# One of three phase additions moved from VectorE to GpSimd in a two-layer attention and gMLP kernel, with eight more units on VectorE

## The chip, the core and the metric

The kernel runs on one core of one Trainium2 chip. The core has TensorE (matmuls; it writes PSUM, a memory of 8 banks of 128 x 512 fp32), ScalarE (activation functions), VectorE and GpSimd (elementwise work; GpSimd reads and writes SBUF alone) and SyncE, which issues the DMAs here. Each engine has its own instruction queue and works through it in order; semaphores order the engines against each other. The metric is the device time of one execution in microseconds (us). Three runs of the kernel before took 1680.24, 1680.46 and 1686.99 us; the median is 1680.46.

## The reference

Two layers, each an attention block (A) and a gMLP block (B), on x of 2048 rows by 512. There are 32 heads of 16 channels, and all heads share one K and one V (multi-query attention).

```python
def _A_ref(x, wq, wk, wv, wo):
    q = (x @ wq).reshape(B, S, H, Dh).transpose(0, 2, 1, 3)     # H = 32, Dh = 16, S = 2048
    k = x @ wk
    v = x @ wv
    scores = jnp.einsum('bhqd,bkd->bhqk', q, k) * Dh ** (-0.5)
    p = _softmax(scores, axis=-1)
    o = jnp.einsum('bhqk,bkd->bhqd', p, v)
    return o.transpose(0, 2, 1, 3).reshape(B, S, H * Dh) @ wo

def _B_ref(x, w_in, w_sp, b_sp, w_out):
    z = _gelu(jnp.einsum('bsd,df->bsf', x, w_in))
    z1 = z[..., :Fh].copy()
    z2 = _layernorm(z[..., Fh:], axis=-1)
    g = jnp.einsum('ts,bsf->btf', w_sp, z2) + b_sp[None, :, None]
    return jnp.einsum('bsf,fd->bsd', z1 * g, w_out)

x = x + _A_ref(_layernorm(x), ...); x = x + _B_ref(_layernorm(x), ...)   # twice
```

The attention takes an exponential of 2 x 32 x 2048 x 2048 scores. That is the bulk of the work.

## The kernel before

**Units and blocks.** In each layer the queries and heads are cut into 32 groups (`GROUPS`), each with 512 columns of query and head times 4 row strips j of the PE array. A group runs over 16 key tiles of 128 keys. One group with one key tile is a *unit*: four *blocks* of 128 keys x 512 columns of scores.

**Units on ScalarE.** Most units go the plain way. TensorE makes scores into one of two slots of PSUM, of three and of two banks (`push_slot`, L837). ScalarE takes the exponential of a whole slot, 128x1536 or 128x1024, into the tile `P_ring` (L863). TensorE multiplies with V and adds up into bank 6 (L882).

**Units on VectorE.** The other units, `ON_DVE` counts them per group, are spread through the slots (`plan`, `apart`) and made by VectorE without an exponential (`block_dve`, L951). TensorE writes one block into a side bank (5 or 7). VectorE evacuates it as int16: the score, plus a bias, clipped at 0, is read as the bits of a bf16, which is a rough power of two (L970, four times a unit, into row r0 of the tile `big`). To make it smoother, five such numbers with different offsets (*phases*) are averaged. The first is r0 itself. The other four are r0 with an integer added: VectorE adds for r2 (L981, 128x2048), then for r1 and r3 in one instruction from r0 and r2 (L983, 128x4096), and last for r4 (L985, 128x2048). TensorE then multiplies each phase with V, scaled by that phase's weight, onto the same bank 6 (`sum_units`, L1001, five times four matmuls a unit, in the order of phases 0, 2, 1, 3, 4). The rows of `big` go round a ring of six (`NRING`), five to a unit, so a unit's additions overwrite rows that the unit before it filled, and wait until TensorE has read them.

**Other work.** At the end of a group VectorE evacuates bank 6 (L1059, or L1050 and L1056 with a partial sum), and turns, divisions (L1031 on VectorE, the products L1041 mostly on GpSimd), the output projection and its addition to X (L1089) follow; then layer norms (L737, L738, L742, with GpSimd's L724 and L726 for the reciprocal square root), the gMLP's input projection (L1181, L1206), the GELUs on ScalarE (L1216, L1245, L1177, L1203), the spatial mixing (L1307, L1349, products L1354 on VectorE or GpSimd). TensorE also gets filler matmuls on zeros (L671, L663) where it would stand idle. At the start of layer 1 there is a stretch in which keys, values and the first queries of the new layer are made (`ln_tiles`, `kv_tiles`, `q_slot`, evacuated by VectorE on L759, L777, L810).

**What sets the order.** Every operation is recorded with an engine, a cost in us, a priority and what it reads and writes. `_Graph.schedule` then plays the program through with these costs, as a list scheduler: an engine that is free takes the ready operation with the lowest priority number. What comes out is a fixed order for each engine's queue; semaphore waits are put in from the reads and writes. So a cost in the code changes no duration, only the order. The phase additions have priority 6.98 (`P_PH`), late among VectorE's work, the evacuations L970 have 0.2 (`P_R`), the multiplications with V have 1. The table `URGENCY` adds small numbers to the priorities of named portions of the program ("unit.0.13 pe" is TensorE's part of the VectorE units while pass 13 of layer 0 is open).

Of the kernel before, what the change touches and what calls it, by code (L numbers as in the profile page):

```python
# [6 lines left out]
FP32 = mybir.dt.float32  # L7
# [39 lines left out]
    "/b_front.0.0.4": -2, "/b_front.0.0.4 pe": 2, "/b_front.0.15.1/ln_tiles.0.15.1": -2, "/b_front.0.6.2 pe": 2,  # L47
    "/b_front.0.8.4/ln_tiles.0.8.4": 0.5, "/b_front.0.8.4/norm_z2.0.6.2": -1.5, "/b_front.0.8.4/norm_z2.0.8.4": -2,
    "/b_front.1.12.3 pe": 1.5, "/b_front.1.15.1/ln_tiles.1.15.1": -1.5, "/b_front.1.4.2 pe": -2,
    "/b_front.1.6.2 pe": 1, "/b_front.1.8.4/ln_tiles.1.8.4": 1, "/finish_group.0.1": 3, "/finish_group.0.2": -3,  # L50
    "/finish_group.0.26": -2, "/finish_group.0.29 pe": -1, "/finish_group.0.30 pe": 0.5, "/finish_group.0.31": 3,
    "/finish_group.1.11": -3, "/finish_group.1.27": -3, "/finish_group.1.28 pe": -3, "/finish_group.1.29 pe": 2,
    "/finish_group.1.30 pe": -3, "/finish_group.1.31 pe": 3, "/kv_tiles.0.2.2 pe": 1, "/kv_tiles.1.12.4 pe": -2,
    "/kv_tiles.1.2.2 pe": 1.5, "/kv_tiles.1.4.2 pe": 1, "/kv_tiles.1.6.2": -3, "/kv_tiles.1.6.2 pe": 1,
    "/kv_tiles.1.8.4 pe": 3, "/ln_tiles.0.6.2": -1, "/ln_tiles.1.0.2 pe": -2, "/ln_tiles.1.2.2 pe": -1,
    "/ln_tiles.1.6.2 pe": -1.5, "/ln_tiles.1.8.4 pe": -2, "/mix_late.1.0.2 pe": -3,
    "/mix_late.1.0.2/add_to_x.1.3": -3, "/mix_late.1.0.6": -3, "/mix_stage.0.0.1 pe": -1.5,
    "/mix_stage.0.1.2 pe": -1, "/mix_stage.0.1.3 pe": -1.5, "/mix_stage.1.0.1 pe": -3, "/mix_stage.1.1.3 pe": 0.5,
    "/q_slot.0.11.4 pe": 2, "/q_slot.0.15.4 pe": 1, "/q_slot.0.4.4 pe": -2, "/q_slot.1.12.4 pe": -1.5,
    "/q_slot.1.13.4 pe": 1, "/q_slot.1.15.4 pe": -1.5, "/q_slot.1.3 pe": 2, "/q_slot.1.4.4 pe": -3,  # L60
    "/q_slot.1.8.4 pe": -3, "/turn_tile.1.14.3 pe": 2, "/wo_tiles.0.14.1 pe": -3, "/wo_tiles.0.2.2 pe": -2,
    "/wo_tiles.1.12.2 pe": -2, "/wo_tiles.1.4.2 pe": -3, "/wo_tiles.1.6.2 pe": -2, "unit.0.10 pe": 1,
    "unit.0.11": -2, "unit.0.12 pe": -2, "unit.0.14 pe": -1, "unit.0.16 pe": 3, "unit.0.18 pe": 2,
    "unit.0.23 pe": -3, "unit.0.25 pe": 3, "unit.0.28 pe": -1.5, "unit.0.29": 1, "unit.0.29 pe": 0.5,
    "unit.0.31 pe": -2, "unit.0.33 pe": 1.5, "unit.0.35": -1.5, "unit.0.35 pe": -3, "unit.0.4": -2,
    "unit.0.40 pe": -0.5, "unit.0.9": -1.5, "unit.1.56": 1.5, "unit.1.58": -1, "unit.1.58 pe": 1, "unit.1.59": -1,
    "unit.1.60 pe": -3, "unit.1.62 pe": 3, "unit.1.63 pe": 1, "unit.1.64 pe": -2, "unit.1.65 pe": 1,
    "unit.1.66 pe": -2, "unit.1.67 pe": -1.5, "unit.1.68": -0.5, "unit.1.68 pe": -2, "unit.1.69 pe": -1,
    "unit.1.70": 1.5, "unit.1.71 pe": 1, "unit.1.72 pe": 1, "unit.1.74 pe": 1.5, "unit.1.75 pe": -3,
    "unit.1.77 pe": 1, "unit.1.79 pe": 2, "unit.1.80 pe": 2, "unit.1.83 pe": 0.5, "unit.1.85 pe": 0.5,  # L70
# [423 lines left out]
def bass_interleave_layers__grouped_kv_mqa__mixer_gmlp__prompt_kernel(  # L494
# [46 lines left out]
    mhalf = G.sb([P, 1], FP32, "mhalf")  # L541
    X = G.sb([P, NT, D], BF16, "X")
# [177 lines left out]

    def rstd(n, ve, rs, mv, i0, ni, per_tile, prio):

        for a, b in ([(i, i + 1) for i in range(i0, i0 + ni)] if per_tile else [(i0, i0 + ni)]):
            op("pool", lambda e, a=a, b=b: e.tensor_scalar(ve[:, a:b], mv[:, a:b, 1], LN_EPS, None, op0=ALU.add),  # L724
               0.25, r=[("mv" + n, i) for i in range(a, b)], w=[("ve" + n, i) for i in range(a, b)], prio=prio)
            op("pool", lambda e, a=a, b=b: e.tensor_tensor(rs[:, a:b], ve[:, a:b],  # L726
                                                           mhalf[:, 0:1].to_broadcast([P, b - a]), ALU.pow),
               0.3 + 0.2 * (b - a), r=[("ve" + n, i) for i in range(a, b)] + ["mhalf"],
               w=[("rs" + n, i) for i in range(a, b)], prio=prio)

    @portion
    def ln_tiles(t0, n, xT, keys, per_tile, prio=5, by_dma=False):
# [19 lines left out]
        while t < t0 + n:  # L752
            m = 1 if per_tile else min(2, t0 + n - t)
            tk = _Task()
            products(tk, m * KD, lambda e, k, t=t, tk=tk: e.transpose(  # L755
                bank16(tk.bank)[:, k * P:(k + 1) * P], xn[:, (t + k // KD) % CT, (k % KD) * P:(k % KD + 1) * P],
                ident[:]), lambda k, t=t: [("xn", (t + k // KD) % CT), "ident"], prio, 0.065, per=8)
            c0 = (t if xT is xnTA else t % CT) * P
            dve(lambda e, c0=c0, m=m, tk=tk: e.tensor_copy(  # L759
                xT[:, :, c0:c0 + m * P].rearrange("p kd (t q) -> p t kd q", q=P),  # L760
                bank16(tk.bank)[:, 0:m * KD * P].rearrange("p (t kd q) -> p t kd q", t=m, kd=KD)),
                0.16 + 0.27 * m, [tk], [x for y in range(t, t + m) for x in keys(y)], prio)
            t += m
# [3 lines left out]
    def kv_tiles(t0, n, pr, pr_v):  # L767
# [8 lines left out]
        for a in range(2):  # L776
            dve(lambda e, a=a: e.tensor_scalar(kT_rep[:, a, t0 * P:t0 * P + w], bank32(t1.bank)[:, 0:w], rows[:, a:a + 1],  # L777
                                               None, op0=ALU.mult), 0.15 + 0.135 * n, [t1, "rows"],
                [("K", a, t) for t in range(t0, t0 + n)], pr + 0.05 * a)
# [15 lines left out]
    @portion  # L795
    def q_slot(si, pr=3):

        t0, n, g = GROUPS[2 * si]
        m, w = CT // n, n * P
        tk = _Task()  # L800

        def mk(e, k):
            u, kd = k // KD, k % KD
            c = g // 2 * m + u
            mul = side4 if n > 1 else PE_FULL
            return mul(e, bank32(tk.bank)[:, u * w:(u + 1) * w], wq_r[:, kd, c * P:(c + 1) * P],
                       xnTA[:, kd, t0 * P:t0 * P + w], kd == 0, kd == KD - 1)
        products(tk, m * KD, mk, lambda k: [("xa", k % KD, t) for t in range(t0, t0 + n)] + ["wq"], pr,
                 us=w * MM + 0.01, mode=2 if n > 1 else 0)
        dve(lambda e: e.tensor_scalar(qT[:, si % NQ, :], bank32(tk.bank), Q_SCALE, None, op0=ALU.mult), 0.69, [tk],  # L810
            [("q", si % NQ)], pr)
# [92 lines left out]
    spread = {"todo": [], "summed": []}  # L904

    def plan(passes):

        at = main["n"] + len(main["blocks"])
        for no, (hg, kts, on_dve) in enumerate(passes):
            n = 4 * (len(kts) - len(on_dve))  # L910
            for d, kt in enumerate(on_dve):
# [3 lines left out]
                                       "first": None, "summed": False})  # L915
# [15 lines left out]
    def tiles_free(x):  # L931
# [7 lines left out]
        return all(phr["owner"].get(r, {"summed": True})["summed"] for r in need)  # L939

# [10 lines left out]
    def block_dve(x, j, slot_op):  # L951
# [25 lines left out]
        if k == 3:  # L977
# [7 lines left out]
            dve(lambda e: e.tensor_scalar(ph16[:, r4, :], ph16[:, r0, :], float(PH_A[4]), None, op0=ALU.add), 0.63, base,  # L985
                BIG(r4), P_PH)
# [58 lines left out]

    def evac_first(hg):
        dve(lambda e: e.tensor_copy(acc[:, hg, :], bank32(PVB)), 0.69, ["pvb"], [ACC(hg)], 0)

    def evac_add(hg):
        dve(lambda e: e.tensor_tensor(acc[:, hg, :], bank32(PVB), acc[:, hg, :], ALU.add), 0.69, ["pvb", ACC(hg)],  # L1050
            [ACC(hg)], 0)

    def evac_last(gi, with_acc):
        par = grp["n"] % 2
        if with_acc:
            dve(lambda e: e.tensor_tensor(oT[:, par, :], bank32(PVB), acc[:, gi, :], ALU.add), 0.69,  # L1056
                ["pvb", ACC(gi)], [("oT", par)], 0)
        else:
            dve(lambda e: e.tensor_copy(oT[:, par, :], bank32(PVB)), 0.69, ["pvb"], [("oT", par)], 0)  # L1059
# [43 lines left out]
    def attn_first(t0, n, on_dve):  # L1103

        plan([(q_of(gi), range(t0, t0 + n), [t0 + k for k in on_dve]) for gi in range(NFIRST)])
        for gi in range(NFIRST):
# [10 lines left out]
    def attn_rest():  # L1117
        plan([(q_of(gi), range(NT), UNITS[ON_DVE[now['layer']][gi]]) for gi in range(NFIRST, len(GROUPS))])
        for gi in range(NFIRST, len(GROUPS)):
# [5 lines left out]
    def group_done(gi, with_acc):  # L1125
# [3 lines left out]
        if gi == NFIRST - 1:  # L1129
# [100 lines left out]
    def gelu_rest():  # L1230
# [11 lines left out]
        for t0, n in Z1_LATE:  # L1242
# [4 lines left out]
            us = 0.0  # L1247

# [114 lines left out]
    def sums_lead(n, chain):  # L1363
# [38 lines left out]
    LATE4 = 4  # L1402
    TURN_US = 7.0
# [6 lines left out]
    NFIRST = 2 * CHUNKS[0][1]  # L1410
    ATT = (((0, 2), (2, 6), (8, 8)), ((0, 2), (2, 2), (4, 2), (6, 2), (8, 8)))
    FIRST_DVE = ({2: (2,), 8: (2, 4)}, {8: (3, 5)})
# [10 lines left out]
    ON_DVE = [[0] * NFIRST + [int(c) for c in s] for s in (  # L1423
        "4344433443423243434344233232",
        "4344443434333433344432333231")]

    for layer in range(2):
        now["layer"] = layer
        phr["base"] = 8 - NRING
        for t0, n in KEYS:  # L1430
# [11 lines left out]
            for a0, an in ATT[layer]:  # L1442
                if a0 + an == t0 + n:
                    attn_first(a0, an, FIRST_DVE[layer].get(a0, ()))
# [42 lines left out]
```

## Time and profile before

| | |
|---|---|
| Median of 3 runs | 1680.46 us |
| Profiled execution | 1682.92 us, span of its instructions 1680.1 us |
| Granted TensorE clock, mean | 0.984 |
| ScalarE: first exponential begins | 13.14 us |
| ScalarE: last GELU ends | 1630.05 us |
| Longest waits of ScalarE for scores | 24.0 and 8.3 us, at 802 and 841 us (start of layer 1) |
| Units on VectorE | 202 (808 evacuations of one block) |
| Blocks on ScalarE | 3,288, in 1,316 exponentials |
| Table loads on ScalarE | 14 of 1.283 us |
| GpSimd products L1041, 128x128 | 112 of 0.40 us median, longest 1.26 |

An instruction is named by its line (a helper's line stands for all that calls it), its engine, its operation, and out<-in by tile and shape. PE is TensorE's matmuls, PEld its weight loads, DVE VectorE, ACT ScalarE, POOL GpSimd. A row of a group ends with its busy time, the mean duration of one, and the idle time of the engine just before them with what ended it. A row of a stretch gives, after its start and end, length and busy time of PE, PEld, DVE, ACT and POOL with counts, then the granted clock and the DMA's share. A row in order of time has start and duration first.

### The profile page before, as it was taken

Reading aid. Unit: us, or ns where it says so; the run is one execution under the profiler, and the core shown is the slowest. Engines: PE = TensorE matmul, PEld = TensorE weight load, DVE = VectorE, ACT = ScalarE, POOL = GpSimd, SP = SyncE. Lnnn points to the kernel's source line nnn. Section 1 sums busy time; section 2 is a strip of 40 time slices with the busy share of each in tenths; the row PEclk is TensorE's granted clock in tenths of the full one; section 3 lists DMA queues with packets and bytes.
Section 4 is the critical chain, followed back from the end, with each engine's and each line's share of the span. In section 5 each row is a group of like instructions: output and inputs, shape, how many; then the busy total and the mean of one; then the engine's idle time right before and its main releaser. Section 6 shows DMA issues by size and latency. Waiting matters only on the chain.

```text
span 1680.1 us, 45324 instructions
## 1 busy us (share of the span) xinstructions
PE 1599.8 (95%) x20268; PEld 530.8 (32%) x20281; DVE 1465.9 (87%) x2384; ACT 1563.2 (93%) x1360; POOL 156.6 (9%) x261
## 2 busy tenths in 40 slices
PE   8999999989999998999999999999999999999999
PEld 3222222233333322334532222223333333323344
DVE  8899999997899998877878998999989999887677
ACT  7899999999999999999479999999999999999970
POOL 2000010000000010000430100000110000010012
PEclk9899999999999998999998999999999999989999
DMA  6100010002311230444511100100013203215555
GB/s 186 23 14 14 8 23 8 20 9 76 80 27 43 81 63 17 126 143 141 156 46 23 18 8 11 23 8 14 11 58 74 48 31 83 73 36 142 171 162 146
DMA packets 173266, 102.70 MB, mean 61 GB/s; under 512 B 135056, under 2 KB 145680, under 8 KB 173072
## 3 DMA queue, kind: packets, MB, share of 16 engines
q1 hardware_dynamic: 173072, 99.81, 23.2%
q8 instruction: 158, 2.59, 0.7%
q14 instruction: 36, 0.29, 0.1%
HBM read 36.34 MB, written 31.46 MB: 40 GB/s over the span
## 4 chain that ended last, share of the span: by engine, by line
ACT 80%; PE 17%; DVE 2%; issue 0%; POOL 0%; DMA 0%; SPq 0%; ACTq 0%
ACT P_ring L863 78%; PE ps_all L637 4%; PE ps_all L631 4%; PE ps_all L837 4%; PE ps_all L1001 2%; PE ps_all L882 2%; ACT z2n L1216 1%; PE ps_all L671 1%; PE ps_all L663 0%; ACT L863 0%; ACT L1216 0%; DVE big L970 0%; DMA X<-in_A_x_dram 0%; PE ps_all L755 0%; DVE xn L742 0%
## 5 line engine op out<-in xcount | busy, mean ns | idle before, releaser
L863 ACT ACTIVATE P_ring<-ps_all 128x1536 bf16<-128x1536 f32 (+1 forms) x1316 | 1493.6, 1347 | 63.3 <-PE ps_all L837 62.5
L837 PE MATMUL ps_all<-qT,kT_rep 32*128 32x512 bf16 x4096 | 612.7, 389 | 65.5 <-ACT P_ring L863 54.0
L970 DVE TENSOR_SCALAR big<-ps_all 128x512 int16<-128x512 f32 x808 | 535.4, 685 | 79.3 <-PE ps_all L837 73.0
L837 PEld LDWEIGHTS ps_all<-qT,kT_rep 32*128 32x128 bf16 x4096 | 150.7, 91 | 609.0 <-ACT P_ring L863 496.5
L1001 PE MATMUL ps_all<-big,V_ph 128*32 128x512 bf16 x4040 | 337.4, 388 | 2.7 <-DVE big L985 1.3
L882 PE MATMUL ps_all<-P_ring,V_aug 128*32 128x512 bf16 x3288 | 306.6, 390 | 1.9 <-DVE oT L1059 1.6
L983 DVE TENSOR_SCALAR big<-big 128x4096 int16<-128x4096 int16 x202 | 246.3, 1219 | 5.2 <-PE ps_all L1001 4.7
L1041 POOL TENSOR_TENSOR o_norm<-o_rows,rden 128x128 bf16<-128x128 bf16 x112 | 57.4, 532 | 1010.3 <-DVE rden L1031 973.7
L981 DVE TENSOR_SCALAR big<-big 128x2048 int16<-128x2048 int16 x202 | 138.4, 685 | 5.8 <-PE ps_all L1001 3.6
L985 DVE TENSOR_SCALAR big<-big 128x2048 int16<-128x2048 int16 x202 | 137.9, 692 | 3.1 <-PE ps_all L1001 2.7
L1001 PEld LDWEIGHTS ps_all<-big,V_ph 128*32 128x32 bf16 x4040 | 90.5, 95 | 133.3 <-issue 66.8
L882 PEld LDWEIGHTS ps_all<-P_ring,V_aug 128*32 128x32 bf16 x3288 | 80.9, 95 | 143.8 <-issue 106.8
L637 PE MATMUL ps_all<-xnTA,z2n 128*32 128x512 bf16 x1344 | 95.5, 386 | 0.0
L671 PE MATMUL ps_all<-ones,zeros 128*32 128x512 bf16 x1076 | 94.5, 395 | 0.0
L1089 DVE TENSOR_TENSOR X<-ps_all,X 128x512 bf16<-128x512 f32 x64 | 44.0, 687 | 25.1 <-PE ps_all L637 15.2
L637 PE MATMUL ps_all<-w_in_r,xo 128*32 128x448 bf16 x960 | 62.9, 355 | 0.1
L724 POOL TENSOR_SCALAR ve<-mv 128x1 f32<-128x1 f32 (+3 forms) x40 | 17.3, 434 | 458.8 <-DVE mv L738 355.1
L637 PE MATMUL ps_all<-xo,w_in_r 128*32 128x512 bf16 (+2 forms) x1120 | 57.3, 327 | 0.3 <-DVE big L970 0.2
L1307 DVE TENSOR_TENSOR big<-ps_all,big 128x512 f32<-128x512 f32 x56 | 38.3, 686 | 21.3 <-PE ps_all L637 20.7
L1181 DVE CAST z2n<-ps_all 128x448 bf16<-128x448 f32 x60 | 37.2, 621 | 14.4 <-PE ps_all L637 13.7
L1354 POOL TENSOR_TENSOR z1c<-big,z1c 128x512 bf16<-128x512 f32 (+1 forms) x47 | 45.5, 983 | 36.4 <-DVE big L1349 35.7
L637 PE MATMUL ps_all<-z1c,z2n 128*32 128x512 bf16 x672 | 48.1, 382 | 0.1
(96 smaller groups left out, 1032.7 us busy)
## 6 DMA issues: line engine op xcount, KB each, us to landing
gp_scratch<-big SPq DMA_DIRECT2D x112, 256.0 KB, 2.0
big<-gp_scratch SPq DMA_DIRECT2D x98, 256.0 KB, 3.3
big<-gp_scratch SPq DMA_DIRECT2D x28, 128.0 KB, 2.7
out_dram<-X SPq DMA_DIRECT2D x16, 128.0 KB, 1.7
w_in_r<-in_B_w_in_dram SPq DMA_DIRECT2D x1, 1792.0 KB, 7.3
X<-in_A_x_dram SPq DMA_DIRECT2D x3, 512.0 KB, 6.5
bsp<-in_B_b_sp_dram SPq DMA_DIRECT2D x8, 128.0 KB, 3.5
w_out_r<-in_B_w_out_dram SPq DMA_DIRECT2D x1, 896.0 KB, 5.0
```

What stands on the lines that cost most here:

```text
L631: return e.matmul(out, w, mv, start=start, stop=stop)
L637: ins = e.matmul(out[32 * j:32 * j + 32, :], w[:, 32 * j:32 * j + 32], mv, tile_position=(0, 32 * j), start=start, stop=stop)
L671: ins = e.matmul(bank32(PVB)[32 * j:32 * j + 32, :], zeros[:, 0:32], mv, tile_position=(0, 32 * j), start=False, stop=False)
L837: return e.matmul(out, kT_rep[32 * j:32 * j + 32, a, u[1] * P:(u[1] + 1) * P], qT[32 * j:32 * j + 32, q, :], tile_position=(32 * j, 0), st ...
L863: return e.activation(P_ring[:, s0:s0 + n, :], bank32(b0, n).rearrange("p (k q) -> p k q", k=n), ACTF.Exp, scale=E_SCALE)
L882: ins = e.matmul(bank32(PVB)[32 * j:32 * j + 32, :], V_aug[:, kt, :], P_ring[:, s, :], tile_position=(0, 32 * j), start=first, stop=last)
L970: o = dve(lambda e: e.tensor_scalar(ph16[:, tiles[0], j * QC:(j + 1) * QC], bank32(tk.bank), PH_BIAS, 0.0, op0=ALU.add, op1=ALU.max), 0.66 ...
L981: dve(lambda e: e.tensor_scalar(ph16[:, r2, :], ph16[:, r0, :], float(PH_A[2]), None, op0=ALU.add), 0.63, base, BIG(r2), P_PH)
L983: dve(lambda e: e.tensor_scalar(two_rows(tiles[1], tiles[3]), two_rows(r0, r2), float(PH_A[1]), None, op0=ALU.add), 1.16, base + BIG(r2), ...
L985: dve(lambda e: e.tensor_scalar(ph16[:, r4, :], ph16[:, r0, :], float(PH_A[4]), None, op0=ALU.add), 0.63, base, BIG(r4), P_PH)
L1001: ins = e.matmul(bank32(PVB)[32 * j:32 * j + 32, :], V_ph[:, a, kt, :], big[:, tiles[a], j * QC:(j + 1) * QC], tile_position=(0, 32 * j), ...
L1041: op("pool" if on_pool else "dve", lambda e, b0=b0, nb=nb, dst=dst: e.tensor_tensor(dst, src()[:, b0:b0 + nb, :, 0:DH], rden[:, par, b0:b0 ...
```

## The change

- The last addition of a unit (row r4) is put on GpSimd instead of VectorE where the group's index is under 30 (`POOL_TO`), except for every 99th unit (`POOL_EVERY`); it is given to the scheduler with a cost of 5.0 us (`POOL_US`) and priority 4. 200 of 210 are moved.
- The counts in `ON_DVE` change: 3 units more in layer 0 and 5 in layer 1 are on VectorE, 8 in all, so 32 blocks fewer go through ScalarE's exponential.
- At the start of layer 1, the evacuations for the first two row tiles (two turned inputs, two of K, two of Q; `evac` with `ON_ACT`) are made by ScalarE as copies with a scale instead of by VectorE.
- `URGENCY` is another table throughout (125 entries in place of 101).
- Rewritten without another effect here: `attn_first` takes the range of its groups as arguments, `part_sums` names where partial sums lie (the first four groups alone, as before), `DUMMY` is off.

In the program built from the changed source, the last GELU of z2 in layer 0 and the late GELUs of z1 stand together, with 12 table loads on ScalarE. Lines move: L970 is now L991, L981 L1002, L983 L1004, L985 L1007, L863 L877, L837 L851, L1001 L1024.

```diff
+    def evac(t0, own, us, r, w, prio, dst, src, scale=None):
+
+        if own and t0 in ON_ACT[now["layer"]]:
+            op("act", lambda e: e.activation(dst(), src(), ACTF.Copy, scale=1.0 if scale is None else scale()), us - 0.1,
+               r=r + ["exp_table"] if DUMMY else r, w=w, prio=prio)
+        elif scale is None:
+            dve(lambda e: e.tensor_copy(dst(), src()), us, r, w, prio)
+        else:
+            dve(lambda e: e.tensor_scalar(dst(), src(), scale(), None, op0=ALU.mult), us, r, w, prio)
...
+    def on_gpsimd(x):
+
+        pool_n["n"] += 1
+        gi = x["gi"]
+        return gi < POOL_TO and pool_n["n"] % POOL_EVERY != 0
...
-            dve(lambda e: e.tensor_scalar(ph16[:, r4, :], ph16[:, r0, :], float(PH_A[4]), None, op0=ALU.add), 0.63, base,
-                BIG(r4), P_PH)
+            on_pool = on_gpsimd(x)
+            op("pool" if on_pool else "dve", lambda e: e.tensor_scalar(ph16[:, r4, :], ph16[:, r0, :], float(PH_A[4]), None,
+                                                                       op0=ALU.add), POOL_US if on_pool else 0.63,
+               r=base, w=BIG(r4), prio=4 if on_pool else P_PH)
...
+    DUMMY = False
+    POOL_US, POOL_EVERY, POOL_TO = (5.0, 99, 30)
+    ON_ACT = ((), (0,))
...
-        "4344433443423243434344233232",
-        "4344443434333433344432333231")]
+        "4444433443324343442444332332",
+        "4344444444343443434434333230")]
```

## The prediction

> **What bounds the kernel now.** I read the page's busy shares and its chain of waits first, then the groups, then who waits for whom, then busy time by stretch.
>
> ```profile
> span 1680.1 us, 45324 instructions
> PE 1599.8 (95%) x20268; PEld 530.8 (32%) x20281; DVE 1465.9 (87%) x2384; ACT 1563.2 (93%) x1360; POOL 156.6 (9%) x261
> ...
> ACT 80%; PE 17%; DVE 2%; issue 0%; POOL 0%; DMA 0%; SPq 0%; ACTq 0%
> ...
> L863 ACT ACTIVATE P_ring<-ps_all 128x1536 bf16<-128x1536 f32 (+1 forms) x1316 | 1493.6, 1347 | 63.3 <-PE ps_all L837 62.5
> L970 DVE TENSOR_SCALAR big<-ps_all 128x512 int16<-128x512 f32 x808 | 535.4, 685 | 79.3 <-PE ps_all L837 73.0
> L983 DVE TENSOR_SCALAR big<-big 128x4096 int16<-128x4096 int16 x202 | 246.3, 1219 | 5.2 <-PE ps_all L1001 4.7
> L981 DVE TENSOR_SCALAR big<-big 128x2048 int16<-128x2048 int16 x202 | 138.4, 685 | 5.8 <-PE ps_all L1001 3.6
> L985 DVE TENSOR_SCALAR big<-big 128x2048 int16<-128x2048 int16 x202 | 137.9, 692 | 3.1 <-PE ps_all L1001 2.7
> ```
>
> The chain is ScalarE's exponentials (L863). TensorE's 95% holds the fillers of L671 (94.5 us), which nobody waits for. ScalarE's whole wait for scores is 62.5 us, of which 11.1 is the start and 24.0 and 8.3 are the change of layers; only 19.1 us is scattered.
>
> ```profile
> ACT P_ring L863 <- PE ps_all L837: 62.5, 29, 24.0
> ```
>
> ```profile
> 95.00:360.00 265.00, 250.73 (x3073) 76.06 (x3076) 248.51 (x383) 264.83 (x235) 16.16 (x32) 1.00 0.08 14
> 920.00:1200.00 280.00, 264.09 (x3269) 79.77 (x3270) 262.88 (x401) 278.04 (x245) 20.84 (x32) 0.99 0.08 14
> ```
>
> Here ScalarE (fourth busy time) is at 99% and VectorE (third) at 94%. So VectorE has 6% to spare there: lateness on it soon becomes lateness of TensorE and then of ScalarE.
>
> **What is removed from ScalarE.** Eight units are 32 blocks of 128x512. L863 holds 3,288 blocks in 1493.6 us, 0.454 us each: -14.5 us. The changed order holds 12 table loads for 14, because the last GELU of layer 0 now stands beside the other GELUs: 2 x 1.283 = -2.6 us. Six copies come to ScalarE (at the start of layer 1), 0.59 us each by the GELU row of the same shape (L1203, 592 ns), in place of VectorE's 0.69. They lie in the 24.0 us wait, where ScalarE is idle; the exponential's table load now stands behind them. Together I take 0, bounds -1 and +1.3 (one load bare). Without further effects: 1680.1 - 14.5 - 2.6 = 1663.0.
>
> **VectorE and TensorE.** 192 of 202 last additions leave VectorE: 192 x 0.692 = -132.9 us. Eight units bring 4 x 0.685 + 0.685 + 1.219 = 4.64 each, +37.2. The six copies leave: -3.2. VectorE: 1465.9 - 98.9 = 1367 us. TensorE gets 160 phase matmuls more and 32 others fewer, of which four run at once: 128 x 0.388 / 4 = +12.4 us, covered by the fillers; bare, 12.4 is the price. The new urgencies reorder VectorE and TensorE: I take 0, with the scattered 19.1 us as the bound both ways. What stands behind the additions in GpSimd's queue (112 products of L1041, 40 pairs of L724 and L726) may come one addition later. GpSimd idles 973.7 us ahead of L1041, whose results go to transposes, not to the exponentials; VectorE waited only 7.6 us in all for L726. Cost 0 under that cover, and once per pair, 40 x 2 = 80 us, on VectorE without it.
>
> **How long an addition takes on GpSimd.** No row shows it. Bounds:
>
> ```profile
> L1354 POOL TENSOR_TENSOR z1c<-big,z1c 128x512 bf16<-128x512 f32 x26 | 31.7, 1228 | 28.1 <-DVE big L1349 28.0
> L1354 POOL TENSOR_TENSOR z1c<-big,z1c 128x256 bf16<-128x256 f32 x21 | 13.8, 679 | 8.3 <-DVE big L1349 7.6 <-DVE mv L738 0.6
> ...
> L706 POOL MEMSET V_ph<- 128x2560 bf16 x1 | 2.2, 2231 | 0.1
> ...
> L704 POOL MEMSET V_aug<- 128x512 bf16 x1 | 0.5, 524 | 0.0
> ```
>
> The memsets grow by (2231 - 524) / 2048 = 0.83 ns an element: 1.80 us for 2048. The products, undisturbed 1154 and 667 ns, by 1.90 ns with 0.18 fixed: 4.07 us. A product reads two tensors and the addition one; half the slope gives 0.18 + 2048 x 0.95 = 2.13 us, nearer to the memset. I take 2.13. GpSimd is then busy 156.6 + 426 us, far from full. (The Trainium skill, GPSIMD Engine Reference, Engine selection, calls one-input work "roughly line-rate": an estimate of 1.71 us at its 1.2 GHz, 1.9 with the fixed part, and by the steps below 1685. Its Elementwise table has 4497 ns for a two-input 2048: 1942 by the same steps. No run here shows either yet.)
>
> **What it does to VectorE meanwhile.**
>
> ```profile
> 862.27 1.16 POOL L1354 TENSOR_TENSOR z1c<-big,z1c 128x512 bf16<-128x512 f32 x1
> 862.33 1.24 DVE L742 TENSOR_SCALAR xn<-X,mv,rs 128x512 bf16<-128x512 bf16 x1 [0.25 <-POOL rs L726]
> ```
>
> ```profile
> 48.22 1.23 DVE L983 TENSOR_SCALAR big<-big 128x4096 int16<-128x4096 int16 x1
> 48.36 1.72 POOL L724 TENSOR_SCALAR ve<-mv 128x4 f32<-128x4 f32 x1 [15.36 <-DVE mv L738]
> 49.36 0.69 DVE L985 TENSOR_SCALAR big<-big 128x2048 int16<-128x2048 int16 x1
> ```
>
> L742 has a median of 0.41 us; begun just after a GpSimd product it took 1.24 and ended 0.15 behind it. L724, 0.23 otherwise, took 1.72 when L983 and L985 ran back to back, and ended with them. L970, which reads PSUM, never took over 0.694 beside GpSimd. So whoever of the two starts first on SBUF-to-SBUF work keeps the other out, to the end of what it runs. (The longest such hold here is 1.16 us. For 2 us there is only the Trainium skill, SBUF — State Buffer, Who interferes with whom: held for the whole instruction. Freed in pieces, it would be 1663, a rival below.)
>
> The remaining additions (r2 and r1/r3, now L1002 and L1004) are such work. GpSimd starts 0.09 us behind the VectorE instruction that it waits for, VectorE's next one at once. Of 200 GpSimd additions, 175 wait in the program for the unit's last evacuation by name. Walking VectorE's order behind each, back to back (0.085 off each duration: two L970 take 1.29): in 60, L1002 and L1004 stand first, hold GpSimd off, and evacuations follow; no loss. In 65 something else stands first, GpSimd starts, and L1002 (three times L758 or L1299) is shut out: behind one evacuation by 0.09 + 2.13 - 0.60 = 1.62. In 35, L1002 stands first and evacuations before L1004: behind two, by 0.60 + 2.13 - 1.80 = 0.93. With two odd ones, 102 are late by 1.41 on the mean; for all 200, 165 us. VectorE: 1367 + 165 = 1532 (91%), more than before.
>
> Behind a shut-out L1002 or L1004 stand the next evacuations (L991), for whose PSUM banks TensorE waits, and behind TensorE's wait its next scores. TensorE's own new wait, the fifth phase's matmuls for GpSimd, is laid out for 5.0 us; 1.9 us held off and 2.13 of work are 4.03, cost 0; with a 4.07 us addition it is 1 us late.
>
> What of it reaches ScalarE: over the whole trace TensorE reads a phase 0.84 us (median; quartiles 0.55 and 1.59) after L981 or L983 ends, and scores are ready 0.30 us (median) before their exponential starts. By medians 1.41 - 0.84 - 0.30 = 0.27 x 102 x 200/175 = 31 us; over the spread of both, 60 us. The middle, 46, less the 13% in which VectorE is idle anyway: +40. **Sum: 1663 + 40 = 1703 us.** The profiled span, 1680.1, is 0.4 below the median of the runs, 1680.46, which I neglect. With 1.80 for an addition the same steps give +16, 1679.
>
> **Rivals.** *The additions fall between (faster).* If the blocking is brief, or the evacuations wait for TensorE (73.0 us did) until GpSimd is done, lateness stays under 0.84 + 0.30 and nothing reaches ScalarE: 1663. For it: 60 of 175 are safe by order, and additions are laid out at 5.0 us, so TensorE's fifth phase has room. Against: 102 are not safe, and L742 was held to the end. It decides while the mean lateness is under 1.14. *The addition is as slow as a product (4.07 us).* Then 159 of 175 are late by 2.57. In the long stretch of each layer (all but its first four groups), ScalarE has 1282 us of exponentials, VectorE 1048 of its own work and 439 of waits: VectorE becomes the bound by 205: 1868. It decides from where the waits pass 1282 - 1048 = 234 us, an addition of about 2.7 us. Against: only one tensor is read.
>
> **Chances.** Forecast (1689 to 1760) 0.40; VectorE as the bound, over 1760, 0.20; the additions fall between, under 1672, 0.30; between these, with additions near memset speed, 0.10. A change under 0.5% (1672.1 to 1688.9) can't be told from none. So faster 0.30, same 0.10, slower 0.60. The range: 1658 (1663 less some of the scattered waits) to 1800 (an addition near 3 us: +140 by the spread of both), which leaves out most of the 1868 case. Of the likeliest case alone: 1689 to 1760.
>
> **What would show it.** GpSimd's addition: 2.1 us undisturbed, up to 1.9 longer behind L1002 and L1004. L1002 and L1004 with a second peak 0.9 to 1.6 us above 0.685 and 1.219, VectorE's busy time near 1530, not 1367. ScalarE's waits for scores outside start and change of layers up from 19 to about 60 us, spread over both layers. I am wrong if L1002 and L1004 keep their durations, if the addition takes over 2.7 us, or if VectorE is late and ScalarE still never waits.

## The result, and the profile after

| | before | after |
|---|---|---|
| Median (4 runs each) | 1683.72 us (1680.24 to 1688.01) | 2598.73 us (2595.86 to 2603.96) |
| Ratio, 95% interval | | 1.5436 (1.5383 to 1.5489) |
| Span of the profiled execution | 1680.1 us | 2597.5 us |
| Granted TensorE clock, mean | 0.984 | 0.791 |

The changed kernel takes half as long again. The forecast, 1703 us with a range up to 1800, had the direction, and that GpSimd's addition keeps VectorE's out, but not the size.

The page of the changed kernel: span, busy time by engine, the chain of waits by engine, and the five groups that answer to those shown of before (L877 was L863, L991 was L970, L1002 was L981, L1004 was L983; L1007 on GpSimd is the moved L985).

```profile
span 2597.5 us, 45675 instructions
...
PE 1949.6 (75%) x20343; PEld 559.4 (22%) x20356; DVE 2148.5 (83%) x2234; ACT 1607.7 (62%) x1351; POOL 1310.9 (50%) x461
...
DVE 38%; PE 36%; POOL 5%; issue 3%; ACT 2%; DMA 0%; DVEq 0%
...
L877 ACT ACTIVATE P_ring<-ps_all 128x1536 bf16<-128x1536 f32 (+1 forms) x1303 | 1537.3, 1246 | 903.6 <-PE ps_all L851 896.9
L1007 POOL TENSOR_SCALAR big<-big 128x2048 int16<-128x2048 int16 x200 | 1132.7, 5665 | 886.3 <-DVE big L991 627.5
...
L1004 DVE TENSOR_SCALAR big<-big 128x4096 int16<-128x4096 int16 x210 | 735.4, 3502 | 17.8 <-PE ps_all L1024 14.6
L991 DVE TENSOR_SCALAR big<-ps_all 128x512 int16<-128x512 f32 x840 | 554.6, 683 | 217.1 <-PE ps_all L851 212.4
...
L1002 DVE TENSOR_SCALAR big<-big 128x2048 int16<-128x2048 int16 x210 | 370.6, 1765 | 31.5 <-POOL big L1007 27.3
```

ScalarE's 80% of the chain has become 2%: the chain now goes to and fro between VectorE and TensorE. ScalarE's wait for scores rose from 62.5 to 896.9 us. An addition on GpSimd takes 5.67 us on the mean. VectorE's two remaining additions have grown from 0.685 to 1.765 us (L1002) and from 1.219 to 3.502 (L1004), with the same shapes; the evacuations L991, which read PSUM, have not grown (683 ns, before 685).

Six lines of the changed kernel in order of time, VectorE and GpSimd alone; first the start, then the duration in us.

```profile
995.13 5.36 POOL L1007 TENSOR_SCALAR big<-big 128x2048 int16<-128x2048 int16 x1
995.26 5.77 DVE L1002 TENSOR_SCALAR big<-big 128x2048 int16<-128x2048 int16 x1 [1.94 <-POOL big L1007]
...
1001.07 1.23 DVE L1004 TENSOR_SCALAR big<-big 128x4096 int16<-128x4096 int16 x1
...
1006.01 0.69 DVE L1002 TENSOR_SCALAR big<-big 128x2048 int16<-128x2048 int16 x1
...
1006.06 5.87 POOL L1007 TENSOR_SCALAR big<-big 128x2048 int16<-128x2048 int16 x1 [5.57 <-DVE big L991]
...
1006.74 6.27 DVE L1004 TENSOR_SCALAR big<-big 128x4096 int16<-128x4096 int16 x1
```

In the first unit GpSimd begins 0.13 us ahead of L1002. L1002 needs 0.69 us alone and takes 5.77; it ends 0.54 behind GpSimd, and L1004, which now has VectorE to itself, takes its usual 1.23. In the second unit L1002 begins first and keeps its 0.69, GpSimd is ready 0.05 us later, gets in when L1002 is done, and it is L1004 that is kept out, for 6.27 us instead of 1.22. So each of these two units loses 5.1 us, nearly a whole GpSimd addition, on the one instruction or on the other. Over the whole trace, what VectorE's SBUF-to-SBUF instructions took above their undisturbed durations (those of the same shapes before) is 760 us in 201 instructions (61 L1002, 124 L1004, 16 others), for 200 additions on GpSimd, 3.8 us an addition on the mean. I call this the *hold* below, and give it for each experiment.

The waits of the changed kernel (in total, times, longest, in us) show how it reaches ScalarE:

```profile
ACT P_ring L877 <- PE ps_all L851: 896.9, 469, 11.9
...
PEld ps_all L1024 <- DVE big L1004: 290.7, 103, 6.0
```

TensorE stands in its fixed order before the phase matmuls, because L1004 is late; behind them in its queue are the next scores, and for these ScalarE waits.

### The profile page after: what moved, and what is told of

The parts are those of the page before. It is cut to its first block, busy times and chain, and to the rows that moved or that the text cites. A ratio compares the mean times of both kernels' runs of the same rounds, so it can differ in the third digit from the quotient of the medians.

```text
span 2597.5 us, 45675 instructions
## 1 busy us (share of the span) xinstructions
PE 1949.6 (75%) x20343; PEld 559.4 (22%) x20356; DVE 2148.5 (83%) x2234; ACT 1607.7 (62%) x1351; POOL 1310.9 (50%) x461
## 4 chain that ended last, share of the span: by engine, by line
DVE 38%; PE 36%; POOL 5%; issue 3%; ACT 2%; DMA 0%; DVEq 0%
DVE big L1004 18%; PE ps_all L851 10%; PE ps_all L643 10%; DVE big L1002 9%; PE ps_all L1024 7%; DVE big L991 5%; PE ps_all L896 5%; POOL big L1007 4%; PE ps_all L637 2%; ACT P_ring L877 2%; DVE xn L758 1%; DVE z2n L1299 1%; DVE big L1344 1%; PE ps_all L677 1%; POOL o_norm L1064 0%
## 5 line engine op out<-in xcount | busy, mean ns | idle before, releaser
L877 ACT ACTIVATE P_ring<-ps_all 128x1536 bf16<-128x1536 f32 (+1 forms) x1303 | 1537.3, 1246 | 903.6 <-PE ps_all L851 896.9
L1007 POOL TENSOR_SCALAR big<-big 128x2048 int16<-128x2048 int16 x200 | 1132.7, 5665 | 886.3 <-DVE big L991 627.5
L851 PE MATMUL ps_all<-qT,kT_rep 32*128 32x512 bf16 x4096 | 701.2, 465 | 157.9 <-DVE big L991 97.1
L1024 PE MATMUL ps_all<-big,V_ph 128*32 128x512 bf16 x4200 | 455.6, 491 | 413.5 <-DVE big L1004 249.7
L1004 DVE TENSOR_SCALAR big<-big 128x4096 int16<-128x4096 int16 x210 | 735.4, 3502 | 17.8 <-PE ps_all L1024 14.6
L991 DVE TENSOR_SCALAR big<-ps_all 128x512 int16<-128x512 f32 x840 | 554.6, 683 | 217.1 <-PE ps_all L851 212.4
L896 PE MATMUL ps_all<-P_ring,V_aug 128*32 128x512 bf16 x3256 | 372.5, 470 | 44.0 <-DVE oT L1092 24.2
L1002 DVE TENSOR_SCALAR big<-big 128x2048 int16<-128x2048 int16 x210 | 370.6, 1765 | 31.5 <-POOL big L1007 27.3
L851 PEld LDWEIGHTS ps_all<-qT,kT_rep 32*128 32x128 bf16 x4096 | 146.7, 94 | 817.2 <-issue 351.6
L1024 PEld LDWEIGHTS ps_all<-big,V_ph 128*32 128x32 bf16 x4200 | 101.2, 104 | 623.0 <-DVE big L1004 290.7
L1064 POOL TENSOR_TENSOR o_norm<-o_rows,rden 128x128 bf16<-128x128 bf16 x112 | 77.7, 713 | 94.4 <-DVE rden L1054 93.3
L643 PE MATMUL ps_all<-z2n 128*32 128x512 bf16 x672 | 60.8, 462 | 5.4 <-DVE big L1344 5.4
```

The source lines that it names most:

```text
L643: ins = e.matmul(out[32 * j:32 * j + 32, :], w[:, 32 * j:32 * j + 32], mv, tile_position=(0, 32 * j), start=start, stop=stop)
L851: return e.matmul(out, kT_rep[32 * j:32 * j + 32, a, u[1] * P:(u[1] + 1) * P], qT[32 * j:32 * j + 32, q, :], tile_position=(32 * j, 0), st ...
L877: return e.activation(P_ring[:, s0:s0 + n, :], bank32(b0, n).rearrange("p (k q) -> p k q", k=n), ACTF.Exp, scale=E_SCALE)
L896: ins = e.matmul(bank32(PVB)[32 * j:32 * j + 32, :], V_aug[:, kt, :], P_ring[:, s, :], tile_position=(0, 32 * j), start=first, stop=last)
L991: o = dve(lambda e: e.tensor_scalar(ph16[:, tiles[0], j * QC:(j + 1) * QC], bank32(tk.bank), PH_BIAS, 0.0, op0=ALU.add, op1=ALU.max), 0.66 ...
L1002: dve(lambda e: e.tensor_scalar(ph16[:, r2, :], ph16[:, r0, :], float(PH_A[2]), None, op0=ALU.add), 0.63, base, BIG(r2), P_PH)
```

## The experiments

Two theories of the 915 us. *The hold*: GpSimd keeps VectorE's SBUF-to-SBUF additions out for as long as it moves data. *Lateness*: GpSimd's result itself comes too late, since 5.4 us of work was laid out as 5.0, and TensorE and VectorE wait for it. A third thing has to be taken off first: the new units, urgencies and copies, which came with the change. Before took 1677.33, 1677.68 and 1681.27 us beside the three groups of runs. `e_tiny` was run 9 times, `e_off`, `e_words` and `e_words_before` 4 times, the others once.

### A shorter addition in the same order

```diff
-            op("pool" if on_pool else "dve", lambda e: e.tensor_scalar(ph16[:, r4, :], ph16[:, r0, :], float(PH_A[4]), None,
+            op("pool" if on_pool else "dve", lambda e, n=2 if on_pool and whole(x) else 2048: e.tensor_scalar(ph16[:, r4, 0:n], ph16[:, r0, 0:n], float(PH_A[4]), None,
```

This is the edit of `e_tiny`; the others have 512, 1024 or 1536 in place of the 2. `whole` leaves 4 of the 200 additions as they were (they are in the means below). The other columns of row r4 keep older values, so these kernels leave out part of the fifth phase. Every engine's instructions, their order and their waits are those of the changed kernel: VectorE's 2,234 and ScalarE's 1,351 instructions stand in the same order in the traces.

> 196 of GpSimd's 200 additions write 2 columns instead of 2048 (the rest of row r4 keeps older values); every instruction of the other four engines and its waits are those of the changed kernel. Theory A, GpSimd's 5.36 us addition holds VectorE's SBUF-to-SBUF instructions off (759 us in all): an addition takes about 0.25 us, VectorE's time above its undisturbed durations falls from 759 to under 40 us, the time to 1655 to 1690. Theory B, TensorE waits for GpSimd's late fifth phase: the same time, but then the run with long GpSimd work and little data stays slow. Theory C, the new order, units and urgencies are slow by themselves: over 2400.

> The same with 512 of 2048 columns: 0.1 + 512 x 2.57 ns = 1.4 us an addition. Theory A: a unit's held time falls from 3.8 us by about 3.9, to a few tenths: under 120 us in all, time 1670 to 1750. Theory B: as with 2 columns. Theory C: over 2400.

> The same with 1024 columns: 2.75 us an addition. Theory A: held time 3.8 - 2.6 = 1.2 us a unit, about 240 us in all; time 1780 to 1950. Theory B: 2.75 is well under the 5.0 laid out, so 1655 to 1690. Theory C: over 2400.

> 196 of the GpSimd additions write 1536 of 2048 columns (4.06 us). Theory A1 with a limit at 1024 columns: held time some 2 us a unit, 400 us in all, time 1900 to 2250. Theory A3, no limit, a smooth growth of held time from 0.3 (512) over 0.7 (1024): about 1.1 us a unit, time 1740 to 1790. Theory B, lateness alone: 4.06 is under 5.0, 1685 to 1720.

| columns | GpSimd, mean us | hold, us | clock | time, us |
|---|---|---|---|---|
| 2 (`e_tiny`, 9 runs) | 0.64 | 20 | 0.991 | 1684.97 |
| 512 (`e_quarter`) | 2.20 | 55 | 0.988 | 1688.27 |
| 1024 (`e_half`) | 3.37 | 109 | 0.988 | 1715.91 |
| 1536 (`e_1536`) | 4.41 | 559 | 0.832 | 2321.69 |
| 2048 (the change) | 5.67 | 760 | 0.791 | 2598.73 |

With next to nothing to add, the same plan in the same order runs at 1.004 (1.0017 to 1.0063) of before. Its page, the chain and two groups (L1016 is GpSimd's addition, L1013 what was L1004):

```profile
ACT 73%; PE 23%; DVE 3%; DMA 0%; issue 0%; POOL 0%; SPq 0%
...
L1016 POOL TENSOR_SCALAR big<-big 128x2 int16<-128x2 int16 (+1 forms) x200 | 127.8, 639 | 913.4 <-DVE big L1000 626.4
...
L1013 DVE TENSOR_SCALAR big<-big 128x4096 int16<-128x4096 int16 x210 | 261.8, 1247 | 6.2 <-PE ps_all L1033 2.6
```

ScalarE is the chain again and L1013 is back at 1247 ns. So the plan costs next to nothing, and all but some 8 us come from what GpSimd's instruction does. It does not grow evenly with the columns: up to 1024 the time rises by 31 us, from 1024 to 1536 by 606, while the mean duration rises by a third. My ranges for 1024 (1780 to 1950) and for 1536 (1900 to 2250) both missed: the first run came out faster and the second slower, since I had the hold grow more evenly (240 and 400 us).

### As long, but with hardly any data

```diff
-            op("pool" if on_pool else "dve", lambda e: e.tensor_scalar(ph16[:, r4, :], ph16[:, r0, :], float(PH_A[4]), None,
...
+            if on_pool and whole(x):
+                op("pool", lambda e: e.tensor_tensor(big[:, r4, 0:64].bitcast(FP32), phw[:, 0:1].to_broadcast([P, 32]), mhalf[:, 0:1].to_broadcast([P, 32]),
+                                                     ALU.pow), POOL_US, r=base + ["mhalf", "phw"], w=BIG(r4), prio=4)
```

> 196 additions are replaced by a power of 32 elements, which takes GpSimd about 0.4 + 32 x 0.156 = 5.4 us with hardly any data (row r4 gets 64 columns of it, the rest keeps older values); the other engines' instructions and waits are unchanged. Theory A in the form that the data hold the port: VectorE's held time under 60 us, time 1655 to 1760 (results 0.4 us later than laid out). Theory A in the form that any GpSimd instruction holds it from start to end: about 2600. Theory B: about 2600, since the fifth phase is as late as before. Theory C: over 2400.

A power of 32 elements keeps GpSimd for 5.64 us on the mean, as long as the addition, and reads and writes almost nothing. It took 1786.88 us, 27 above my range (1655 to 1760), with a hold of 25 us, most of it in the four additions left whole. One stretch of its trace has both kinds: L1017 is the power (two here, back to back), L1020 one of the four additions left whole, L1011 and L1013 are what was L1002 and L1004.

```profile
996.94 12.46 POOL L1017 TENSOR_TENSOR big<-phw,mhalf 128x32 f32<-128x32 f32 x2
...
1003.44 0.69 DVE L1011 TENSOR_SCALAR big<-big 128x2048 int16<-128x2048 int16 x1
...
1004.17 1.23 DVE L1013 TENSOR_SCALAR big<-big 128x4096 int16<-128x4096 int16 x1
...
1009.38 5.37 POOL L1020 TENSOR_SCALAR big<-big 128x2048 int16<-128x2048 int16 x1
...
1009.51 5.78 DVE L1011 TENSOR_SCALAR big<-big 128x2048 int16<-128x2048 int16 x1 [1.28 <-POOL big L1017]
```

Beside the power VectorE runs at 0.69 and 1.23; beside the addition, 5 us later, at 5.78. In the whole trace 343 of VectorE's L1011 and L1013 run beside a power and none of the whole additions; the worst loses 0.13 us. So it is not GpSimd being busy that holds VectorE, but GpSimd moving data. What the power does cost is lateness, as its waits show:

```profile
DVE big L1011 <- POOL big L1017: 101.5, 89, 4.6
PEld ps_all L1037 <- POOL big L1017: 97.5, 123, 2.8
```

That divides the 914 us between the changed kernel and `e_tiny`: 1786.88 - 1684.97 = 102 us for lateness, 2598.73 - 1786.88 = 812 us for the hold. The 812 us include what comes with the hold, the lower clock too. The division is that of this order of taking away: in the changed kernel itself VectorE is so late that only 27.3 + 20.4 + 14.4 = 62 us of wait are put down to GpSimd's result.

### All of it on VectorE

```diff
-    POOL_US, POOL_EVERY, POOL_TO = (5.0, 99, 30)
+    POOL_US, POOL_EVERY, POOL_TO = (5.0, 99, 0)
```

> All last additions are back on VectorE, all else of the change stays; the order is made anew with VectorE's 0.63 us. Theory A, the whole loss is GpSimd's addition: 1660 to 1690. Theory C, the eight units and the urgencies cost by themselves: over 1720.

1726.25 us, 1.0287 (1.0249 to 1.0324) of before, with a hold of 7 us. My range (1660 to 1690) missed, and the time lies in the rival's (over 1720). The eight more units and the copies without GpSimd's help are 49 us slower than before. It does not show that the units and urgencies cost this much anywhere: `e_tiny` has both and took 8 us more than before. Here the scheduler makes the order anew, with urgencies that were not made for it: ScalarE, still 66% of the chain, idles 62.6 us between the first and the last exponential of layer 1 (before 19.1). Any kernel below in which a cost or a place changes carries such a part; it is not a clean measure of one thing.

### Two shorter additions

```diff
+            def halves(e):
+                for c in (0, 1024):
+                    ins = e.tensor_scalar(ph16[:, r4, c:c + 1024], ph16[:, r0, c:c + 1024], float(PH_A[4]), None, op0=ALU.add)
+                return ins
...
+    POOL_US, POOL_EVERY, POOL_TO = (6.6, 99, 30)   # e_split_long alone; e_split keeps 5.0
```

> The changed kernel with each GpSimd addition issued as two instructions of 1024 columns, nothing left out; the other engines' instructions and waits are unchanged. Theory A1, the hold depends on the length of one instruction: VectorE's held time per unit some 0.7 to 1.5 us, 150 to 300 us in all, time 1790 to 1950 (the power run's lateness, about 100, plus that). Theory A2, the hold goes by the whole of the data: about 2600.

> The changed kernel with the addition as two int16 additions of 1024 columns (2.76 to 4.2 us each when laid out at 5.0 in the run before, where it took 1909.8 us with 122 us of VectorE held and TensorE and VectorE waiting some 320 us for GpSimd), now laid out at 6.6 us, so that the order of the work reckons with about what they take; the order of all engines is remade. Theory (most of what the two halves cost is that their result comes later than laid out): waits for GpSimd fall to under 150 us and the time to 1730 to 1830. Rival (the cost is the hold and the length itself, wherever it is laid out): 1880 to 1930.

`e_split`, in the changed kernel's order, took 1909.8 us: 689 less than the change with the same numbers computed, since each half is short enough to let VectorE in (hold 122 us). GpSimd needs 2 x 3.16 us a unit, though, and waits for its result came to 115 us on VectorE and 203 on TensorE and its weight loads. Laid out at 6.6 us (`e_split_long`) the time is 1901.9, hardly less. That was the rival's number, not mine. The waits for GpSimd's result did fall, as I had it (to 16 us on TensorE and 86.5 on VectorE), but the time did not, and the chain still holds GpSimd:

```profile
PE 32%; ACT 24%; POOL 23%; DVE 18%; issue 3%; DMA 0%; SPq 0%; DVEq 0%; POOLq 0%
```

With 6.2 us a unit GpSimd is itself a link that sets the time, in both layouts (38% of the chain in `e_split`). How much of this run is the order made anew stays open.

### The two engines by themselves

> No part of the reference's work is done; the input is copied to the output. GpSimd makes integer additions of 256 to 4096 columns, alone and with a VectorE addition of 128x4096 begun 0.7 us later; also bf16, a copy, fp32, and an int32 addition of 1024 words. Theory A1, GpSimd holds the port only while it fetches or stores, and its store comes at the end for short rows: VectorE's addition is 0.3 us late at 512 columns and 0.7 at 1024, as in the runs with 512 and 1024, GpSimd being held off in turn; from some length above 1024 it is late to GpSimd's end (about 4.5 us at 2048). Theory A2, held from start to end at every length: late by GpSimd's time less 0.7 us: 0.7 at 512, 2.0 at 1024, 4.6 at 2048. GpSimd alone: 0.12 + 2.57 ns a column, 10.6 us at 4096.

> A bench of single instructions, not the computation. GpSimd instructions of several kinds and sizes, each with a VectorE addition of 128x4096 (alone 1.23 us) that begins some 0.7 us behind them; then pairs of VectorE additions of 128x2048 (alone 0.69 us each), once independent of each other and once with the second reading the first's result, with a GpSimd addition that becomes ready together with the first. Theory: what decides is the bytes that the GpSimd instruction moves, not its time: 1024 int16 columns (2048 bytes a partition, 2.77 us) let VectorE through, 1024 int32 words (4096 bytes, 1.89 us) did not. Then 256 and 512 words cost VectorE at most 0.3 us and 768 words hold it to the end; 512 fp32 columns cost it at most 0.3 us, 768 and 1024 hold it to the end; of the int16 additions between 1024 and 1280 all above 1024 hold it (about 3.1 us at 1088, 3.3 at 1152, 3.5 at 1216, 3.84 at 1280), and the copy of 2048 columns holds it while that of 1024 does not. Rival: the kind decides, and every int32 instruction of two inputs holds VectorE to its end. The memset (it reads nothing) holds nothing by either. Pairs: in an independent pair both additions take 0.69 us and the GpSimd addition is held off behind both; in a dependent pair the 2048-column GpSimd addition begins in the gap and the second VectorE addition takes about 5.8 us, with the 1024-column one at most 1.5 us. Rival for the pairs: the two behave alike.

Both are programs of single instructions: a GpSimd instruction alone, or with a VectorE addition of 128x4096 (1.23 us alone) that begins 0.68 us behind it. Alone, GpSimd's addition took 0.85 us for 256 columns, 1.49 for 512, 2.77 for 1024, 5.37 for 2048 and 10.54 for 4096: (10.539 - 5.365) / 2048 = 2.53 ns a column; 2048 columns of bf16 (5.36) and 1024 of fp32 (2.77) took as long as those of int16. A copy of 2048 columns took 1.89, and 1024 int32 words added with `tensor_tensor` to one repeated column 1.89 too. Together, of the second program in order of time (L538 is GpSimd's addition, L544 VectorE's):

```profile
9.38 3.01 POOL L538 TENSOR_SCALAR d<-src 128x1024 int16<-128x1024 int16 x1 [8.56 <-DVE small L531]
10.05 1.44 DVE L544 TENSOR_SCALAR d<-src 128x4096 int16<-128x4096 int16 x1
...
16.19 3.12 POOL L538 TENSOR_SCALAR d<-src 128x1152 int16<-128x1152 int16 x1 [0.28 <-DVE small L531]
16.87 3.52 DVE L544 TENSOR_SCALAR d<-src 128x4096 int16<-128x4096 int16 x1
```

At 1024 columns VectorE loses 0.2 us and GpSimd 0.24. At 512 VectorE loses nothing (1.23) although GpSimd began first, and it is GpSimd that takes 2.37 for 1.49; I had expected VectorE 0.3 late at 512 and 0.7 at 1024. At 1152 VectorE is kept out and ends 1.08 us behind GpSimd. 1088 columns let it through (1.49), 1216 and 1280 do not (3.68, 3.84); in the first program it was kept out to 5.76 by 2048 columns and to 10.94 by 4096. My reason for the border, the bytes, fell: 1024 columns of fp32, twice the bytes, let VectorE through (1.44), while 512 and 768 int32 words (1.44, 1.86), a copy of 1024 columns (1.42) and a memset that reads nothing (3.89 for 4096) all kept it out to their own end and 1.08 us more, as the 1152 columns did. So the rival was right that the kind counts; the memset missed both theories. The words and the copy cost VectorE little only because they are short.

For the pairs, too, the rival was right. The same program, two VectorE additions of 128x2048 that do not depend on each other, and a GpSimd addition ready at the same time as the first:

```profile
66.36 0.69 DVE L547 TENSOR_SCALAR d<-src 128x2048 int16<-128x2048 int16 x1
66.41 5.86 POOL L538 TENSOR_SCALAR d<-src 128x2048 int16<-128x2048 int16 x1 [0.28 <-DVE small L561]
66.97 5.85 DVE L550 TENSOR_SCALAR d<-src 128x2048 int16<-128x2048 int16 x1
```

The second VectorE addition is there, 0.08 us before the first one ends, and still GpSimd comes in between. With the second one reading the first one's result it was the same (5.73). VectorE's standing first protects the one instruction that runs, and none behind it.

### Shorter in time

```diff
+            def halves(e):
+                for c in (0, 1024):
+                    ins = e.tensor_tensor(big[:, r4, c:c + 1024].bitcast(I32), big[:, r0, c:c + 1024].bitcast(I32),
+                                          add4[:, 0:1].to_broadcast([P, 512]), ALU.add)
+                return ins
```

Two int16 numbers stand in each word; `add4` holds the constant twice.

> The changed kernel with GpSimd's addition made as two additions of 512 int32 words (two phases in a word) in place of one of 2048 int16 columns; plan and order of all other engines as in the changed kernel. By the bench 1024 words took 1.89 us, so the two should take about 2.0 us together, under the 5.0 laid out: nothing is late. Theory (a short instruction does not hold VectorE to its end): VectorE's SBUF-to-SBUF instructions are lengthened by 40 to 150 us in all, as with 512 and 1024 columns (55 and 109), and the time is 1688 to 1720 us. Rival (every int32 instruction holds VectorE to its end, as the 1024-word one did): some 120 instructions lengthened by 1 to 2 us, 150 to 250 us in all, and a time of 1730 to 1850. If the change's length laid out were itself a cost, it would show here as over 1700 with little held.

> The units, urgencies and ScalarE copies of the kernel before, with the last phase addition of nearly every unit on GpSimd as two additions of 512 int32 words, laid out at 2.6 us. ScalarE does the same work as before, and it has 9.3 and 19.1 us of idle time in the two layers. Theory: ScalarE sets the end, VectorE's relief of about 120 us is not worth more than that idle time: 1668 to 1690 us against 1678, with 40 to 150 us of VectorE held. Rival (VectorE's lateness still sets part of the end, and the hold gives the relief back): 1690 to 1730.

`e_words`, the whole computation in the changed kernel's order, took 1710.91 us, 1.0182 (1.0158 to 1.0206) of before and 888 us less than the change. GpSimd's words took 1.03 us undisturbed, 1.44 on the mean, and the hold was 110 us. Time and hold are in my range, but for another reason than I wrote: by the programs above, words do hold VectorE to their end, and each is over in 1 us. `e_words_before` (the units, urgencies and copies of before) took 1761.62, 1.0482 (1.0454 to 1.0509). Both expectations missed it. Its hold is 101 us; ScalarE idles 31.8 and 61.2 us within the two layers (before 9.3 and 19.1), under urgencies made for another cost. I did not separate the two. No kernel here that computes everything beats the one before.

## Why the prediction was wrong

**The addition on GpSimd: the step that failed.** "A product reads two tensors and the addition one; half the slope gives 0.18 + 2048 x 0.95 = 2.13 us" and the bounds 1.80 to 4.07: measured 5.36 undisturbed, a third above my upper bound. That the addition keeps VectorE out to its end was right, and the size was not; "if the addition takes over 2.7 us" named the case, the rival at 1868 was the nearest, and I gave a time over 1760 a chance of 0.20. The slope of products and memsets says nothing about an addition of a constant: an int32 addition, `tensor_tensor` with a repeated column, adds the same 2048 numbers as 1024 words in 1.89 us, and the form with a constant takes 2.8 times as long. The Trainium skill (GPSIMD Engine Reference, Engine selection) calls one-input work "roughly line-rate"; the copy's 1.89 us agrees with that, the addition's 5.37 does not.

**"in 60, L1002 and L1004 stand first, hold GpSimd off ... no loss".** Wrong. Of the 102 L1004 that run right behind L1002, 59 were held, for 296 us in all. GpSimd comes in between, as in the second unit shown above: in 51 of the 102 its addition became ready while an undisturbed L1002 ran, and L1004 was held in all 51. I had taken this from the L724 of before, which ended with L985. The programs above show that row to be no proof: the addition of 512 columns began first, let VectorE run its 1.23 us and finished behind it, 0.88 us longer than alone. That L724 did so was not tested.

**The hold to the end.** Right for this addition (5.77 us beside 5.36), and the chip's rule is narrower than I put it: it held for 1152 columns and more, for words, copies and memsets, but not for this addition up to 1088 columns. The Trainium skill (SBUF — State Buffer, Who interferes with whom) has it "for the whole instruction": the trace agrees for the first group and not for the last.

**165 us of hold, 40 us on ScalarE.** Measured: 760 of hold, and about 812 of time with it. With 5.36 us, the arithmetic of my rival (159 of 175 late, 2.57 + 1.29 = 3.86 us each, 94% of it in the long stretches) gives 159 x 200 / 175 x 3.86 x 0.94 = 659 us, VectorE the bound by 1048 + 659 - 1282 = 425, and 2088 us. That sum lets VectorE work on without a pause. In fact it stood still for 2597.5 - 2148.5 = 449 us (before 214), 212.4 of it (before 73.0) for scores from a TensorE that was itself waiting for L1004. Two engines that wait for each other in turn take longer than the busier one alone; that is the second thing the sum lacked.

**The result in time for the fifth phase, and GpSimd "far from full".** I gave both nothing. With 5.64 us of work, and nobody held, `e_pow` is 102 us slower than `e_tiny`; GpSimd is busy 1283.0 us (72%) there and 38% of the chain. Both costs hang on the 2.13 us again.

**The clock.** It was no term of mine. The scores' matmul (L851) took 465 ns on the mean, 387 in `e_tiny`, at a granted clock of 0.791 and 0.991. TensorE is 36% of the chain, 935 us; at 387 ns it would be 778, so the clock's own share is some 157 us by this estimate. The clock goes with TensorE's busy share: 0.991 at 94% (`e_tiny`), 0.939 at 88% (`e_split`), 0.832 at 81% (`e_1536`), 0.791 at 75%. In the changed kernel it is at half for 1088 us, in 143 stretches, and in the 3.4 us before such a stretch TensorE was busy 28% of the time on the mean. So in this trace the clock falls behind TensorE's pauses, which speaks for a result of the waits and not their first cause; no run here has the hold without the lower clock.

**What was right.** The exponentials: 1493.6 - 14.5 = 1479.1, measured in `e_tiny` 1478.9 (1537.3 in the changed kernel, where 707 of them begin before the last one has ended, for 1248 in `e_tiny`). The 12 table loads. VectorE's own work: 1367 forecast, 2148.5 - 760 = 1388 measured. L991 untouched. GpSimd held off by VectorE by half a us at the median (5.86 against 5.36) and by 1.1 at most (6.44), within the 1.9 I gave. VectorE's wait for GpSimd's reciprocal square roots (L742): 5.0 us, where I had cost 0 under cover.

**1663 without side effects.** `e_tiny` is this case but for 20 us of hold, and it took 1685. Against the profile of before, ScalarE's first layer is 10.75 us shorter, but the change of layers 3.45 longer (the copies stand in it; my bound was 1.3), layer 1 1.38 longer (its scattered idle time 10.1 us more), and the tail after the last exponential 6.86 longer: together +0.9 where I had -17.1. So even the rival "the additions fall between" would not have come out faster.

## What to carry to other kernels

Before an operation is moved to an engine on which the trace has never shown it, run that very form there, alone and beside its new neighbour: the slopes of other operations were off by 2.5 times. In these runs, work on GpSimd that moves data in SBUF is paid for by VectorE's SBUF-to-SBUF work, so what counts is how long one GpSimd instruction moves data and how much of VectorE's work stays on PSUM; two instructions of 1 us instead of one of 5.4 took 888 us off this kernel. Ask what the plan takes with the moved work at almost no cost, too: here that (`e_tiny`, 1.004 of before) showed that there was nothing to win.

## What the runs showed of the hardware

- GpSimd's addition of a constant takes 2.53 ns a column, as long for 2048 columns of bf16 and 1024 of fp32 as for int16; a copy of 2048 columns takes 1.89 us, an int32 addition of 1024 words 1.89 us.
- Up to 1088 columns such an addition holds VectorE only for a part of its time (when VectorE begins 0.68 us behind it, not at all at 512 and 768 columns, 0.2 us at 1024, 0.26 at 1088); from 1152 on for all of it, by count of elements and not by bytes. Three passes of 0.84 ns a column, VectorE free in the second and GpSimd's third waiting for VectorE to end, would fit: by them GpSimd takes 0.68 + 1.23 + 0.43 = 2.34 us at 512 columns (measured 2.37), 2.56 at 768 (2.58) and 2.95 at 1024 (3.01). That is argued from the numbers, not shown; why it ends between 1088 and 1152 is open.
- A power of 32 elements takes 5.4 us, and VectorE's additions beside it lose 0.13 us at most.
- Of VectorE's work only the instruction that runs is safe from a GpSimd addition of 2048 columns: the next one, ready 0.08 us before the first ends, took 5.85 us instead of 0.69.
